# Windowed attention with a split-precision FFN: other places for the score divisions, the pair loads and the y weight sums

## The chip, the cores and the metric

The kernel runs on one core of one Trainium2 chip. The metric is device time in microseconds (us) of one execution; the time before is the median of three runs. TensorE is called PE (its weight loads PEld), VectorE DVE, ScalarE ACT, GpSimd POOL and the sync engine SP, as in the profile. SP issues every DMA of this kernel from one in-order queue.

## What is computed

```python
# attention: q, k, v are (8, 8, 576, 64)
scores = scale * np.matmul(q, k.transpose(0, 1, 3, 2))
rel = pos[:, None] - pos[None, :]
mask_plain = (rel >= 0) & (rel < 32)                       # heads 0 to 3
mask_dil = (rel >= 0) & (rel < 128) & (rel % 4 == 0)       # heads 4 to 7
attn = exp(scores - max) / (sum + 1e-9);  out = attn @ v
# FFN: x is the attention output as (4608, 512), d_ff is 2048
h = x @ w_in
g = np.maximum(h, 0.0) + alpha * np.minimum(h, 0.0)
y = g @ w_out
```

## The kernel before, in words

Every fp32 product is made of three fp32r matmuls (high·high, high·low, low·high), so each operand needs a high part (a cast, on ACT) and a low part (a subtraction, on DVE). The FFN has 9 token tiles of 512 and 16 blocks `f` of 128 hidden rows. A product of 128x128x512 with its three passes over four chunks is 12 matmuls.

**Slices.** The first three token tiles run in 48 slices, numbered `n` in the two loops of the main program (the second loop starts at L1347). Slice `n` issues on PE `ffn_h` of the next slice (12 matmuls, L488), `ffn_y` of the previous one (12 matmuls, L536), and, where the tables `score_at` and `value_at` name a pair, `scores` (72 small matmuls, L266) and `values` (76, L361) of attention pairs: 32 pairs of batch and two heads, of which pairs 8 to 23 belong to slices 20 to 46. DVE makes `ffn_parts` (L508, L509) and `ffn_low` (L519), the division and transpose of the pair scored one slice earlier (`divisions` L338 to L340, `turns` L346), `maxima` (L318, L321) and half of the evacuation (`lows`, L422); ACT makes `ffn_high` (L514), `exponentials` (L331) and the other half (`highs`, L415). The tiles for k, q and v of a pair have one buffer each, so the load of the next pair (`load_qk` L236/L237, `load_v` L246) can start only when the scores, or the values, of the present one have run.

**Weight sums.** From tile 3 on the FFN uses a seven-product scheme for 2x2 blocks (Strassen-Winograd), which needs sums of weight blocks. They are made ahead, in the slices: `combine` (input weights, eight sums, POOL L586 and L589; cast on ACT L594, low part on DVE L599, two stores L601) and `others` (output weights, POOL L611 and L613; ACT L617, DVE L621, four stores L624). Four of the eight output sums are made in slices; `second_sums` makes the other four later: numbers 4 and 5 on POOL in the first h phase (L1055, L1057, L1065), numbers 6 and 7 on DVE in the y phase behind it. In slices 20 to 35 `save` also stores the split weights, four DMAs a slice.

**Paired stage.** Tiles 3 to 8 run as three pairs of tiles, each in two groups of hidden blocks, so six times an **h phase** (`phase_h`) and a **y phase** (`seven_y`). An h phase has four units `i`; each has the products 1, 7, 6, 2, 5, and while unit `i` runs, the products 3 and 4 of unit `i-1` are put behind its product 1. A product is 6 matmuls (L718). `snap`, `negative` and `high` are ACT's, `add`, `value`, `term` and `low` DVE's. Product 2 of a unit takes the PSUM bank that product 7 and 4 of the unit before filled, so it waits for that unit's `add(21)` on DVE (L770). The hook table of `attention_hooks` puts the last eight pairs into the first four h phases, two into each: a hook `(i, p)` runs behind product `p` of unit `i`. The steps of a pair are scores with maxima, exponentials of five and of four blocks, `middle` (divisions and transpose on DVE), and `end` (values on PE, L308, then evacuation and the store `keep`, L225).

All engines run in the order in which the program is written (a manual schedule); there is no planner.

```python
for u, follows, at in zip(two, (two[1], None), (0, 2)):
    first = (0, 1) if at == 0 else (1, 5)
    hooks[first].append(lambda u=u, follows=follows: scores(u, follows))
    hooks[at, 6].append(lambda u=u: u.exponentials(0, 5))
    hooks[at, 5].append(lambda u=u: u.exponentials(5))
    hooks[at + 1, 4].append(lambda u=u: middle(u))
    hooks[at + 1, 6].append(lambda u=u, follows=follows: end(u, follows))
```

Of the kernel before, what the change touches and what calls it, by code (L numbers as in the profile page):

```python
# [66 lines left out]
def tile_window_attention_prelu_ffn(  # L67
# [528 lines left out]
    def combined_low(i):  # L596
# [3 lines left out]
        for a, w in enumerate((hi, lo)):  # L600
            nc.sync.dma_start(out=wS[i, 3:7, :, a].rearrange("q p n -> p q n"), in_=w.bitcast(F32))  # L601
# [3 lines left out]
    def others(i):  # L605

        sums_of["y"] = t = const.tile([P, 4, 2, 2, P], F32, tag="xA0", name=f"ysum_{i}")
        for j in range(2):
            hi, lo = (
                weight(1, a, 2 * i + j).bitcast(F32).rearrange("p (q c n) -> p q c n", q=2, c=2) for a in range(2))  # L610
            nc.gpsimd.tensor_tensor(out=t[:, 2 * j:2 * j + 2, :, 1], in0=hi, in1=lo, op=ALU.add)  # L611
        for out, x, y, op in ((3, 1, 3, ALU.add), (1, 0, 1, ALU.subtract), (0, 3, 0, ALU.subtract), (2, 2, 0, ALU.subtract)):
            nc.gpsimd.tensor_tensor(out=t[:, out, :, 1], in0=t[:, x, :, 1], in1=t[:, y, :, 1], op=op)  # L613

    def others_high():
        t = sums_of["y"]
        nc.scalar.copy(out=t[:, :, :, 0].bitcast(F32R), in_=t[:, :, :, 1])  # L617

    def others_low(i):
        t = sums_of["y"]  # L620
        nc.vector.tensor_tensor(  # L621
            out=t[:, :, :, 1].bitcast(F32R), in0=t[:, :, :, 1], in1=t[:, :, :, 0], op=ALU.subtract)
        for q in range(4):
            nc.sync.dma_start(  # L624
                out=wY[i, q].rearrange("p c a n -> p (c a n)"), in_=t[:, q].rearrange("p c a n -> p (c a n)"))

    sums_of = {}
# [239 lines left out]
    def phase_h(t, grp, hooks):  # L867
# [15 lines left out]
        for i in range(GP):  # L883
# [12 lines left out]
            u.mm(7)  # L896
            if last:
# [23 lines left out]
    def seven_y(t, grp, us, hooks):  # L921
# [107 lines left out]
    )  # L1029

    def second_sums(in_h, in_y):


        for i, k, loaded, fetches, added, cast, last, stores in SUMS:
            room, to = [], in_h if loaded is None else in_y

            def fetch(c, i=i, k=k, room=room):
                if c == 0 and type(k) is int:
# [468 lines left out]
```

## Time and profile before

| what | value |
|---|---|
| median of 3 runs (lowest, highest) | 920.37 us (919.35, 920.66) |
| the profiled execution | 920.85 us |
| its span, first to last instruction | 918.9 us |
| mean granted TensorE clock | 0.969 of full speed |
| busy: PE, DVE, ACT, POOL | 845.7, 666.7, 453.1, 89.0 us |
| DMA moved | 192.79 MB, 210 GB/s on average |

The profiled execution is 1.95 us longer than its span and 0.48 us above the median. Times inside the trace count from the span's start. Rows of a busy PE do not say that it runs at its peak: what PE lost is read from idle time in front of its instructions and from the granted clock.

### The profile page before, as it was taken

What the parts mean: (1) busy time and instruction counts of PE and PEld (TensorE: products, weight loads), DVE (VectorE), ACT (ScalarE), POOL (GpSimd) and SP (SyncE); (2) the same over time, 40 slices, a digit from 0 to 9 for tenths busy, and PEclk for the clock granted to TensorE, in tenths of its full rate; (3) what the DMA queues carried; (4) which work ended last, traced back from release to release, by engine and by line L of the source; (5) the groups of instructions that cost most, each with busy time, mean ns of one, the idle gap of its engine ahead of it and who ended that gap; (6) DMA issues with size and microseconds to landing.
All of it is one profiled execution on the core that took longest, in us unless ns stands there. A gap on an engine that the chain in (4) does not pass through costs nothing.

```text
span 918.9 us, 20357 instructions
## 1 busy us (share of the span) xinstructions
PE 845.7 (92%) x8014; PEld 687.5 (75%) x8014; DVE 666.7 (73%) x1121; ACT 453.1 (49%) x1240; POOL 89.0 (10%) x88
## 2 busy tenths in 40 slices
PE   7889999989988988977899989898999899999998
PEld 5668888877776777865687778677877788888886
DVE  5987767566676587777775888878457888863894
ACT  7876666344333444455434743564246435642650
POOL 0000000220424464024000000000000000000000
PEclk9999999999999899998899999999999999999999
DMA  7742542387699465685598669765766687666664
GB/s 256 260 167 76 177 164 82 115 294 240 205 292 296 163 224 199 215 292 180 180 317 296 183 191 318 244 178 148 236 194 179 187 288 235 193 194 194 193 188 158
DMA packets 130492, 192.79 MB, mean 210 GB/s; under 512 B 11614, under 2 KB 67550, under 8 KB 130398
## 3 DMA queue, kind: packets, MB, share of 16 engines
q1 hardware_dynamic: 130398, 191.51, 66.1%
q8 instruction: 63, 1.03, 0.5%
q14 instruction: 31, 0.25, 0.1%
HBM read 145.33 MB, written 46.14 MB: 208 GB/s over the span
## 4 chain that ended last, share of the span: by engine, by line
PE 72%; DVE 12%; issue 5%; DMA 5%; ACT 4%; SPq 2%; ACTq 0%; DVEq 0%
PE h L488 13%; PE qA L1016 13%; PE pA L718 11%; PE y L536 10%; PE qC L1016 6%; PE pC L718 5%; PE pB L718 5%; PE qB L1016 3%; PE o L361 3%; PE s L266 2%; DMA q<-qT 2%; DVE parts_w L703 1%; PE o L308 1%; DVE raw_xB L697 1%; DVE py L945 1%
## 5 line engine op out<-in xcount | busy, mean ns | idle before, releaser
L488 PE MATMUL h<-x,w_dt.float32r 128*128 128x512 f32 x576 | 144.7, 401 | 3.6 <-DVE pr L318 2.7
L536 PE MATMUL y<-g,w_dt.float32r 128*128 128x512 f32 x576 | 138.5, 390 | 0.0
L488 PEld LDWEIGHTS h<-x,w_dt.float32r 128*128 128x128 f32 x576 | 109.1, 192 | 27.4 <-DVE pr L318 2.9
L536 PEld LDWEIGHTS y<-g,w_dt.float32r 128*128 128x128 f32 x576 | 108.0, 188 | 22.4
L331 ACT ACTIVATE pr<-pr,nm 128x64 f32<-128x64 f32 x216 | 72.4, 339 | 49.5 <-DVE nm L321 49.5
L763 ACT COPY stage<-pA 128x512 f32<-128x512 f32 x72 | 41.8, 580 | 62.2 <-PE pA L718 60.4
L514 ACT CAST g<-m 128x512 fp32r<-128x512 f32 x48 | 29.7, 619 | 70.8 <-DVE m L509 67.9
L718 PE MATMUL pA<-parts_w,ring_w 128*128 128x512 f32 x234 | 58.4, 392 | 0.0
L827 ACT CAST gp<-held 128x512 fp32r<-128x512 f32 x60 | 36.7, 624 | 43.1 <-DVE held L823 42.4
L718 PE MATMUL pA<-parts_w,ring_xA 128*128 128x512 f32 x222 | 55.6, 394 | 0.2 <-ACT stage L763 0.2
L718 PEld LDWEIGHTS pA<-parts_w,ring_w 128*128 128x128 f32 x234 | 44.2, 190 | 9.6
L718 PEld LDWEIGHTS pA<-parts_w,ring_xA 128*128 128x128 f32 x222 | 42.2, 191 | 9.6 <-ACT stage L763 0.6
L508 DVE TENSOR_SCALAR m<-h,al 128x512 f32<-128x512 f32 x27 | 20.2, 749 | 36.0 <-PE h L488 33.5
L519 DVE TENSOR_TENSOR g<-m,g 128x512 fp32r<-128x512 f32 x48 | 34.3, 715 | 12.5 <-ACT g L514 12.4
L770 DVE TENSOR_TENSOR stage<-pC,stage 128x512 f32<-128x512 f32 x48 | 33.0, 687 | 14.1 <-ACT stage L763 13.8
L777 DVE SCALAR_TENSOR_TENSOR held<-held,bal,stage 128x512 f32<-128x512 f32 x42 | 31.9, 758 | 14.6 <-ACT held L807 14.0
L1016 PE MATMUL qA<-gp,ring_xA 128*128 128x512 f32 x174 | 42.4, 390 | 0.0
L331 ACT ACTIVATION_READ_ACCUMULATOR pr<-pr,nm 128x1 f32 x216 | 41.0, 190 | 0.0
L832 DVE TENSOR_TENSOR gp<-held,gp 128x512 fp32r<-128x512 f32 x60 | 40.3, 679 | 0.0
L941 ACT COPY py<-qA 128x512 f32<-128x512 f32 x24 | 13.8, 587 | 52.2 <-PE qA L1016 48.0
L1016 PE MATMUL qA<-gp,ring_w 128*128 128x512 f32 x162 | 39.5, 389 | 0.0
L308 PE MATMUL o<-lasting_pt,lasting_v 32*64 32x64 f32 (+1 forms) x672 | 11.0, 276 | 30.3 <-issue 20.5
(193 smaller groups left out, 1746.2 us busy)
## 6 DMA issues: line engine op xcount, KB each, us to landing
ring_w<-wS SPq DMA_DIRECT2D x69, 256.0 KB, 2.8
ring_xA<-wS SPq DMA_DIRECT2D x66, 256.0 KB, 3.0
ring_xA<-wY SPq DMA_DIRECT2D x40, 256.0 KB, 2.9
ring_w<-wY SPq DMA_DIRECT2D x36, 256.0 KB, 3.0
ring_g<-wS SPq DMA_DIRECT2D x33, 256.0 KB, 3.0
wO<-w_dt.float32r SPq DMA_DIRECT2D x32, 256.0 KB, 4.4
wS<-wc SPq DMA_DIRECT2D x16, 512.0 KB, 4.1
ring_w<-wO SPq DMA_DIRECT2D x31, 256.0 KB, 3.1
```

Source lines behind the costliest of these rows:

```text
L331: nc.scalar.activation(out=self.pr[:, r, :], in_=self.ps[r // CUT0][:, r % CUT0, :] if self.onto else self.pr[:, r, :], func=AF.Exp, bias= ...
L488: nc.tensor.matmul(ms[t, f], lhsT=weight(0, a, f)[:, c * P:(c + 1) * P], rhs=half(t, c)[:, e, :], start=(c == 0 and n == 0), stop=(c == NC ...
L514: nc.scalar.copy(out=g[:, 0, :], in_=ms[t, f])
L519: nc.vector.tensor_tensor(out=g[:, 1, :], in0=ms.pop((t, f)), in1=g[:, 0, :].bitcast(F32), op=ALU.subtract)
L536: nc.tensor.matmul(ys[t][c], lhsT=weight(1, a, f)[:, c * P:(c + 1) * P], rhs=g[:, e, :], start=(first and n == 0), stop=(last and n == 2),)
L718: nc.tensor.matmul(to, lhsT=w[:, (2 * a + c) * P:(2 * a + c + 1) * P], rhs=part_of(name, e)[:, c * TT:(c + 1) * TT], start=start and c == ...
L763: nc.scalar.copy(out=self.s(n), in_=self.A)
L770: nc.vector.tensor_tensor(out=self.s(n), in0=getattr(self, src), in1=self.s(to), op=ALU.add)
L777: nc.vector.scalar_tensor_tensor(out=self.m[n], in0=self.m[n], scalar=bal[:, f:f + 1], in1=self.at(n), op0=ALU.mult, op1=ALU.add)
L827: nc.scalar.copy(out=self.pair(n)[:, 0], in_=self.whole(n))
L832: nc.vector.tensor_tensor(out=p[:, 1], in0=self.whole(n), in1=p[:, 0].bitcast(F32), op=ALU.subtract)
L1016: nc.tensor.matmul(to(q)[c], lhsT=w[:, k * P:(k + 1) * P], rhs=rhs[:, e], start=(i, q) in firsts and n == 0, stop=i == GP - 1 and n == 2, ...
```

## The change

Four parts. (1) In the h phases, the first pair's `middle` goes from behind product 4 of unit 1 to behind product 1, its `end` from product 6 to product 7; the second pair's scores, exponentials, `middle` and `end` go from (1,5), (2,6), (2,5), (3,4), (3,6) to (1,2), (2,1), (2,6), (2,5), (3,4). The hooks of product 5 now run in front of `negative(11)` and `add(22)`. (2) In the slices, `load_qk` of the next pair is issued directly behind the scores and `load_v` directly behind the values; before, both stood at the end of the slice. `keep` goes to the end of the next slice, the stores of `combine` to the end of their own. (3) `others` makes six of the eight output sums in slices (32, 34, ... 42, cast two slices later) in a tile with two halves; the high part gets a tile of its own from the five that rotate for `g`, the low part is made behind the last exponentials, and the store, now eight DMAs of 128 KB, one slice later. `second_sums` keeps numbers 6 and 7. (4) The eight `combine` slices move from 21, 23, 31, ... 41 to 21, 23, 25, 31, ... 39.

```diff
     def others(i):
-        sums_of["y"] = t = const.tile([P, 4, 2, 2, P], F32, tag="xA0", name=f"ysum_{i}")
+        if not ysums:
+            ysums.append(const.tile([P, 2, 4, 2 * P], F32, tag="xA0", name="ysums"))
+        t = ysums[0][:, len(ysums) % 2]
+        ysums.append(t)
...
+        sums_of[i] = t
+    def others_high(i):
+        high = gbuf([P, 4, 2 * P], F32R, f"wd{i}")
+        nc.scalar.copy(out=high, in_=sums_of[i])
+        sums_of[i] = high, sums_of[i]
     def others_low(i):
+        high, t = sums_of[i]
+        nc.vector.tensor_tensor(out=t.bitcast(F32R), in0=t, in1=high.bitcast(F32), op=ALU.subtract)
+    def others_store(i):
+        for a, t in enumerate(sums_of[i]):
+            for q in range(4):
+                nc.sync.dma_start(
+                    out=wY[i, q, :, :, a], in_=(t if a else t.bitcast(F32))[:, q].rearrange("p (c n) -> p c n", c=2))
...
             u.mm(7)
+            also(7)
...
             u.add(11)
+            also(2)
...
             u.snap(3)
+            also(5)
             u.negative(11)
             u.add(22)
             more(5)
-            also(5)
...
     SUMS = (
-        (4, "xC0", None, ((0, 1), (0, 1), (0, 4), (0, 4)), (1, 1), (2, 1), (2, 1), ((2, 4), (2, 6))),
-        (5, "xC1", None, ((0, 6), (0, 5), (1, 1), (1, 4)), (2, 1), (2, 5), (3, 1), ((3, 4), (3, 6))),
...
+        steps = ((0, 1), (0, 6), (0, 5), (1, 1), (1, 7)), ((1, 2), (2, 1), (2, 6), (2, 5), (3, 4))
...
-    for k, n in enumerate((21, 23, 31, 33, 35, 37, 39, 41)):
+    for k, n in enumerate((21, 23, 25, 31, 33, 35, 37, 39)):
...
-    for k, n in enumerate((32, 35, 38, 41)):
+    for k, n in zip((4, 5, 0, 1, 2, 3), range(32, 44, 2)):
         other_at[n] = cast_at[n + 2] = k
...
         if scored:
             scored.scores()
+            pairs[pairs.index(scored) + 1].load_qk()
         if valued:
             valued.values()
+            pairs[pairs.index(valued) + 1].load_v()
         if n in split_at:
             combined_low(split_at[n])
-        if n in cast_at:
-            others_low(cast_at[n])
+            put[n].append(lambda i=split_at[n]: combined_store(i))
...
-            valued.keep()
+            put[n + 1].append(valued.keep)
         if scored:
             scored.exponentials(5)
-        for u in pairs[2 * NC:AHEAD + 1]:
...
+        if n in cast_at:
+            others_low(cast_at[n])
+            put[n + 1].append(lambda i=cast_at[n]: others_store(i))
...
+        for op in put.pop(n, ()):
+            op()
```

**DVE, second h phase, behind product 5 of unit 0.** `pC` and `stage` are product bank and snapshots, `held` the values, `rs` the inverse row sums, `pr` the exponentials, `lasting_pt` their transpose. Before, from `add(22)` to the transpose:

```order
L770 TENSOR_TENSOR stage_5846<-pC_1_0_5806,stage_5835 128x512
L777 SCALAR_TENSOR_TENSOR held_4975<-held_4975,bal,stage_5835 128x512
L777 SCALAR_TENSOR_TENSOR held_5000<-held_5000,bal,stage_5846 128x512
L777 SCALAR_TENSOR_TENSOR held_5011<-held_5011,bal,pA_1_0_5751 128x512
L770 TENSOR_TENSOR stage_5846<-pC_1_0_5806,stage_5759 128x512
L832 TENSOR_TENSOR split_xB_5013<-held_4975,split_xB_5013 128x512
L777 SCALAR_TENSOR_TENSOR held_5026<-held_5026,bal,stage_5846 128x512
L338 TENSOR_SCALAR rs_2_5887<-sums_79 128x9
L339 RECIPROCAL rs_2_5887<-rs_2_5887 128x9
L340 TENSOR_TENSOR pr_78<-pr_78,rs_2_5887 128x576
L346 STREAM_TRANSPOSE lasting_pt<-pr_78 128x576
```

Now:

```order
L781 TENSOR_TENSOR stage_5869<-pC_1_0_5825,stage_5854 128x512
L338 TENSOR_SCALAR rs_2_5881<-sums_79 128x9
L339 RECIPROCAL rs_2_5881<-rs_2_5881 128x9
L340 TENSOR_TENSOR pr_78<-pr_78,rs_2_5881 128x576
L346 STREAM_TRANSPOSE lasting_pt<-pr_78 128x576
L788 SCALAR_TENSOR_TENSOR held_5023<-held_5023,bal,stage_5854 128x512
L788 SCALAR_TENSOR_TENSOR held_5043<-held_5043,bal,stage_5869 128x512
L788 SCALAR_TENSOR_TENSOR held_5054<-held_5054,bal,pA_1_0_5770 128x512
L781 TENSOR_TENSOR stage_5869<-pC_1_0_5825,stage_5778 128x512
L843 TENSOR_TENSOR split_xB_5056<-held_5023,split_xB_5056 128x512
L788 SCALAR_TENSOR_TENSOR held_5069<-held_5069,bal,stage_5869 128x512
```

The four instructions of the division and transpose stand in front of six others that they stood behind; the second row from the end but one (`add(21)`, from bank `pC`) now stands behind them.

**SP, slice 22** (`ob` is the finished output of tile 1, k_2 and q_2 belong to the pair scored in slice 23). Before:

```order
L549 DMA out<-ob_15_0_2116 128x512
L549 DMA out<-ob_15_1_2117 128x512
L549 DMA out<-ob_15_2_2118 128x512
L549 DMA out<-ob_15_3_2119 128x512
L246 DMA v_1_2238<-vW 128x640
L236 DMA k_2_2240<-kT 128x576
L237 DMA q_2_2241<-qT 128x576
```

Now:

```order
L236 DMA k_2_2170<-kT 128x576
L237 DMA q_2_2171<-qT 128x576
L246 DMA v_1_2214<-vW 128x640
L549 DMA out<-ob_15_0_2116 128x512
L549 DMA out<-ob_15_1_2117 128x512
L549 DMA out<-ob_15_2_2118 128x512
L549 DMA out<-ob_15_3_2119 128x512
```

The three loads stand in front of the four stores, and k and q in front of v.

**POOL, from its last sums of the slices to its end** (`wsum` are input weight sums, `ysum` and `ysums` output weight sums, `wy` the sums of `second_sums`). Before:

```order
L586 TENSOR_TENSOR wsum_xA_3243<-w_3_dt.float32r 128x512 x2
L589 TENSOR_TENSOR wsum_xA_3243<-wsum_xA_3243 128x256 x4
L611 TENSOR_TENSOR ysum_4358<-w_3_dt.float32r 128x4x128 x2
L613 TENSOR_TENSOR ysum_4358<-ysum_4358 128x2x128 x4
L1055 TENSOR_TENSOR wy_4884<-wy_4884 128x8x128
L1057 TENSOR_TENSOR wy_4884<-wy_4884 128x2x128 x4
L1065 TENSOR_TENSOR wy_4884<-wy_4884 128x8x128
L1055 TENSOR_TENSOR wy_4950<-wy_4950 128x8x128
L1057 TENSOR_TENSOR wy_4950<-wy_4950 128x2x128 x4
L1065 TENSOR_TENSOR wy_4950<-wy_4950 128x8x128
```

Now:

```order
L586 TENSOR_TENSOR wsum_xA_3255<-w_3_dt.float32r 128x512 x2
L589 TENSOR_TENSOR wsum_xA_3255<-wsum_xA_3255 128x256 x4
L616 TENSOR_TENSOR ysums<-w_0_dt.float32r 128x512 x2
L619 TENSOR_TENSOR ysums<-ysums 128x256 x4
L616 TENSOR_TENSOR ysums<-w_3_dt.float32r 128x512 x2
L619 TENSOR_TENSOR ysums<-ysums 128x256 x4
```

The instructions on `wy` are gone from POOL, and it ends with the sums of the slices.

## Rows read from the trace of the kernel before

**Rows 1.** The page, busy time, share and instructions of each engine.

```profile
PE 845.7 (92%) x8014; PEld 687.5 (75%) x8014; DVE 666.7 (73%) x1121; ACT 453.1 (49%) x1240; POOL 89.0 (10%) x88
```

**Rows 2.** Waits of PE: engine, line, released by: us in total, times, longest.

```profile
PE o L308 <- issue: 20.5, 5, 4.7
PE s L266 <- DMA q<-qT: 11.9, 5, 3.8
PE o L308 <- DVE lasting_pt L346: 9.8, 3, 5.3
PE pB L718 <- DVE stage L770: 5.4, 4, 4.6
```

**Rows 3.** Stretches of slices 23, 33, 36 to 38, 40, 44: length, busy us, PEclk, DMA.

```profile
core 0: us, PE busy (x) PEld busy (x) DVE busy (x) ACT busy (x) POOL busy (x), PEclk, DMA share, GB/s
180.67:194.03 13.36, 9.60 (x177) 8.11 (x173) 8.91 (x18) 6.97 (x31) 4.64 (x6) 0.87 0.84 279
262.92:275.41 12.49, 9.72 (x177) 8.21 (x173) 9.09 (x18) 5.65 (x26) 4.06 (x5) 0.86 0.91 303
289.45:303.35 13.90, 9.50 (x173) 7.81 (x173) 7.62 (x15) 5.85 (x32) 11.36 (x12) 0.85 0.76 240
303.35:310.18 6.83, 6.83 (x26) 5.53 (x25) 2.95 (x7) 2.39 (x11) 0.00 (x0) 0.80 0.48 158
310.18:318.13 7.95, 7.95 (x173) 6.61 (x171) 7.13 (x11) 2.89 (x5) 5.13 (x4) 1.00 0.73 256
323.71:334.58 10.87, 8.10 (x173) 6.61 (x171) 9.98 (x11) 3.57 (x4) 9.32 (x8) 1.00 0.36 127
353.71:366.24 12.53, 9.00 (x173) 7.56 (x172) 10.63 (x14) 4.61 (x5) 1.14 (x1) 0.91 0.78 275
```

**Rows 4.** Timeline in the slices: start, us, instruction, [idle before it <- releaser].

```profile
178.25 1.21 PE L266 MATMUL s<-k,q 64*32 64x64 f32 x72
...
185.61 0.45 SPq L237 DMA_DIRECT2D q<-qT  x1
...
190.17 2.15 PE L266 MATMUL s<-k,q 64*32 64x64 f32 x72 [3.76 <-DMA q<-qT]
```

**Rows 5.** Stretches of h phases 1 to 5, columns as in rows 3.

```profile
384.75:446.56 61.81, 47.20 (x469) 37.65 (x468) 43.55 (x64) 29.03 (x82) 17.16 (x12) 0.86 0.69 227
...
487.39:536.45 49.06, 42.01 (x469) 33.68 (x468) 34.83 (x67) 27.93 (x85) 0.00 (x0) 0.97 0.65 207
...
577.25:628.78 51.53, 43.65 (x470) 34.81 (x468) 39.14 (x67) 27.92 (x80) 0.00 (x0) 0.93 0.60 184
...
669.58:720.31 50.73, 43.66 (x470) 34.83 (x469) 34.80 (x65) 27.94 (x85) 0.00 (x0) 0.93 0.59 166
...
761.13:797.26 36.13, 35.92 (x158) 29.07 (x157) 29.99 (x45) 21.33 (x38) 0.00 (x0) 1.00 0.73 219
```

**Rows 6.** Timeline of the second h phase, which starts at 487.39, columns as in rows 4.

```profile
502.44 0.17 DVE L338 TENSOR_SCALAR rs<-sums 128x9 f32<-128x9 f32 x1
...
504.57 1.10 PE L308 MATMUL o<-lasting_pt,lasting_v 32*64 32x32 f32 x84 [2.27 <-issue]
...
516.87 1.66 PE L718 MATMUL pB<-parts_w,ring_w 128*128 128x512 f32 x6 [0.27 <-DVE stage L770]
...
521.25 0.69 DVE L770 TENSOR_TENSOR stage<-pC,stage 128x512 f32<-128x512 f32 x1
...
527.02 0.68 DVE L770 TENSOR_TENSOR stage<-pC,stage 128x512 f32<-128x512 f32 x1
...
531.20 1.52 PE L308 MATMUL o<-lasting_pt,lasting_v 32*64 32x32 f32 x84 [4.51 <-issue]
```

**Rows 7.** Timeline of the first h phase, POOL and DVE.

```profile
416.97 2.81 POOL L1055 TENSOR_TENSOR wy<-wy 128x1024 f32<-128x1024 f32 x1
...
417.48 2.84 DVE L823 TENSOR_TENSOR held<-held,held 128x512 f32<-128x512 f32 x1
```

**Rows 8.** Group of instructions: names, shapes, count | busy us, mean ns | idle before.

```profile
L621 DVE TENSOR_TENSOR ysum<-ysum 128x1024 fp32r<-128x1024 f32 x4 | 5.2, 1304 | 0.1
```

More of the change, by code (lines that the diff above doesn't have):

```diff
@@ L1024, in tile_window_attention_prelu_ffn, with second_sums, sums @@
     SUMS = (
[4 rows of a table removed]
-    )
-    def second_sums(in_h, in_y):
-        for i, k, loaded, fetches, added, cast, last, stores in SUMS:
-            room, to = [], in_h if loaded is None else in_y
+        (6, 1, (5, 6, 7, 8), 15, 20, 22, (24, 25)),
+        (7, 3, (10, 11, 12, 13), 20, 22, 24, (27, 28)),
+    )
+    def second_sums(hooks):
+        for i, k, fetches, added, cast, last, stores in SUMS:
+            room = []
             def fetch(c, i=i, k=k, room=room):
-                if c == 0 and type(k) is int:
+                if c == 0:
                     room.extend(gbuf([P, 2, 2, 2, P], F32, f"wy{i}_{n}", k + n) for n in range(2))
-                elif c == 0:
-                    room.append(const.tile([P, NC, 2, 2, P], F32, tag=k, name=f"wy{i}"))
-                n = NC // len(room)
                 nc.sync.dma_start(
-                    out=room[c // n][:, c % n].rearrange("p o a n -> p (o a n)"),
+                    out=room[c // 2][:, c % 2].rearrange("p o a n -> p (o a n)"),
                     in_=wO[i // GP, c, i % GP].rearrange("p o a n -> p (o a n)"))
             def block(room, q):
-                t, a = (room[q % 2], 0) if len(room) == 2 else (room[0], q % 2 * 2)
-                return t[:, a:a + 2, q // 2, 1]
-            engine = nc.gpsimd if loaded is None else nc.vector
-            def sums(room=room, engine=engine):
+                return room[q % 2][:, :, q // 2, 1]
+            def sums(room=room):
                 for t in room:
-                    engine.tensor_tensor(out=t[:, :, :, 1], in0=t[:, :, :, 0], in1=t[:, :, :, 1], op=ALU.add)
+                    nc.vector.tensor_tensor(out=t[:, :, :, 1], in0=t[:, :, :, 0], in1=t[:, :, :, 1], op=ALU.add)
                 for out, x, y, op in ((3, 1, 3, ALU.add), (1, 0, 1, ALU.subtract), (0, 3, 0, ALU.subtract), (2, 2, 0, ALU.subtract)):
-                    engine.tensor_tensor(out=block(room, out), in0=block(room, x), in1=block(room, y), op=op)
+                    nc.vector.tensor_tensor(out=block(room, out), in0=block(room, x), in1=block(room, y), op=op)
             def high(room=room):
@@ L1076, in second_sums @@
             for c in range(NC):
-                to[fetches[c]].append(lambda c=c, fetch=fetch: fetch(c))
-            to[added].append(sums)
-            to[cast].append(high)
-            to[last].append(low)
+                hooks[fetches[c]].append(lambda c=c, fetch=fetch: fetch(c))
+            hooks[added].append(sums)
+            hooks[cast].append(high)
+            hooks[last].append(low)
             for half in range(2):
-                to[stores[half]].append(lambda half=half, store=store: store(half))
+                hooks[stores[half]].append(lambda half=half, store=store: store(half))
     def reload(t, c):
@@ L1125, in end @@
             u.keep()
-        for u, follows, at in zip(two, (two[1], None), (0, 2)):
-            first = (0, 1) if at == 0 else (1, 5)
-            hooks[first].append(lambda u=u, follows=follows: scores(u, follows))
-            hooks[at, 6].append(lambda u=u: u.exponentials(0, 5))
-            hooks[at, 5].append(lambda u=u: u.exponentials(5))
-            hooks[at + 1, 4].append(lambda u=u: middle(u))
-            hooks[at + 1, 6].append(lambda u=u, follows=follows: end(u, follows))
+        steps = ((0, 1), (0, 6), (0, 5), (1, 1), (1, 7)), ((1, 2), (2, 1), (2, 6), (2, 5), (3, 4))
+        for u, follows, at in zip(two, (two[1], None), steps):
+            for n, op in zip(at, (
+                    lambda u=u, follows=follows: scores(u, follows), lambda u=u: u.exponentials(0, 5),
+                    lambda u=u: u.exponentials(5), lambda u=u: middle(u),
+                    lambda u=u, follows=follows: end(u, follows))):
+                hooks[n].append(op)
     def paired_stage():
@@ L1140, in paired_stage @@
                 if (t, grp) == (NSTD, 0):
-                    second_sums(in_h, in_y)
+                    second_sums(in_y)
                 two, todo = todo[:2], todo[2:]
```

43 lines of the change are left out of this document (16 added, 27 removed), and 2 rows, old and new, of the table SUMS.

## Prediction

> **What bounds the kernel now.** I read the busy line first: PE is busy 92% of the span, DVE 73% [rows 1]. So PE is the bound, and a change pays where PE stands idle or runs at half clock. PE's waits [rows 2] name the places. Before the values of the h phases (L308) it waits 20.5 + 9.8 = 30.3 us in eight places, once for each pair of these phases; "issue" there can't be the whole cause, because the transpose that the values read comes late on DVE (below). Before the scores of the slices (L266) it waits 11.9 us for `q`, in five places. Before product 2 it waits 5.4 us for DVE's snapshot (L770).
>
> The windows then tell what a wait costs beyond itself. A clean slice with scores and values takes 7.95 us at PEclk 1.00. Slices 23, 33 and 36 hold the same PE work and take 13.36, 12.49 and 13.90, at 0.85 to 0.87 [rows 3]: behind a gap PE runs for a while at the lower of its two clock levels (1.2 instead of 2.4 GHz), and in rows 3 slice 37, which has no idle time at all (6.83 busy of 6.83), still ran at 0.80. The h phases read the same way: the fifth, without attention, takes 36.13 at 1.00; the first four take 61.81, 49.06, 51.53 and 50.73 at 0.86 to 0.97 [rows 5].
>
> **Part 1, the h phases.** What must PE do in one? The 36.13 of the fifth phase, and two pairs: scores of 1.21 [rows 4] and values of 1.10 [rows 6] each, so 36.13 + 2 x 2.31 = 40.7 us. That is the floor at full clock; the four phases lie 213.13 - 4 x 40.7 = 50.3 above it.
>
> First values, in the second phase (start 487.39) [rows 6]. The division started at 502.44, 15.05 after the start; PE's values ran at 504.57, 2.13 later, after 2.27 idle, so PE was there at 14.91. In the changed order the division stands in front of six DVE instructions of 128x512, 6 x 0.68 = 4.1, so it may start at 10.95 and PE can begin at 13.08. PE gets there one product earlier (1.66 by the product in rows 6), at 13.25. The gap closes, with little to spare.
>
> What is late next is `add(21)`: product 2, at 516.87, waited 0.27 for it. The DVE instructions that stand ahead of it are the same set as before, only in another order, so it comes sooner only as far as DVE had idle time to fill. PE, however, comes 2.27 sooner. Between no such filling (wait 0.27 + 2.27 = 2.5) and full filling (0.3) I take about half: 1.2.
>
> Second values: they ran at 531.20 after 4.51 of idle [rows 6], so PE was there at 526.69, and by the same 2.13 the division had started at 529.07. In the changed order it stands, right behind an `add` of the unit before, eight DVE instructions of 128x512 sooner, next to the one that ran at 521.25. From there 2.13 more is 523.38. PE gets to the values two products sooner, 526.69 - 2 x 1.66 = 523.37, and the 2.27 of the first gap sooner than that, less the 1.2 that it now waits: 522.3. DVE too runs ahead where it waited for PE. I take the gap as gone, and 1.1 as the most that stays. `add(21)` of that unit ended at 527.02 + 0.68 = 527.70; PE arrives at product 2 behind it sooner by about what it saved, and I take another wait of 0.9, by the same bounds of 0.3 and 2.5. At the end the y phase finds DVE's last parts later than PE: nothing to 2, I take 0.9.
>
> So each phase takes 40.7 + 1.2 + 0.9 + 0.9 = 43.7, and the four save 213.13 - 174.8 = **38.3**. The bounds are 46 a phase (both waits at 2.5; saves 29) and the floor (saves 50). By phases that is 18.1, 5.4, 7.8 and 7.0. The first gains most since POOL's 17.16 us of sums [rows 5] leave it: beside a POOL sum of 2.81 a DVE instruction of 128x512, 0.68 elsewhere [rows 6], took 2.84 [rows 7].
>
> **Part 2, the loads.** Before, the scores that free `k` and `q` ended at 178.25 + 1.21 = 179.46, but the `q` load was issued only at 185.61, behind four stores and `v`, and the scores came at 190.17 after 3.76 idle [rows 4]. From issue to use took 4.56. Issued directly behind the scores it would land by about 185; PE wanted it at 190.17 - 3.76 = 186.4. Slices 23, 33 and 36 stand 39.75 - 3 x 7.95 = 15.9 above clean ones [rows 3], waits and clock together; slice 37 loses 6.83 x 0.20 = 1.3 to the clock; the other two waits for `q`, of at most 3.8 each, I put at 2. Of these 19.2 some stay: the window of slice 36 is the longest though `q` cost it no more than 3.8, so other gaps stand in it. Between the bare waits (11.9) and 19.2 I take **16**.
>
> The price of the move: stores and `save` now wait behind loads on SP's queue, and `keep` and the stores of the sums wait a slice. What waits for the stores is a tile that is written again: one slice of about 8 us stands between, and a load took 4.56. The cover is that slice; without it, the price is the fourth rival below.
>
> **Parts 3 and 4, the sums.** Slice 40 takes 10.87 and slice 44 12.53 for the work of 7.95; DVE is busy 9.98 and 10.63 of it, with a low part of 1.30 (L621) in front of the maxima [rows 3, 8]. Behind the last exponentials it no longer holds them: 1.3 in slice 40; in slice 44, 4.6 lost with the clock at 0.91, of which I take 3. Bounds 0 and 7.5; taken **4.3**. Against that stand two more sums in the slices: on POOL two times six instructions, at the 9.32 / 8 of slice 40 [rows 3] some 14 us; on DVE 2 x 1.30 [rows 8]; on ACT two casts of about as much. A clean slice with 5.13 us of POOL beside 7.13 of DVE took 7.95 [rows 3], so DVE and POOL have room there; eleven sums fill nearly every slice from 31 to 42 now. Bounds 0 and 3 (both low parts wholly on the path); taken **1**.
>
> Does POOL hold DVE off? One DVE instruction was stretched by 2.84 - 0.68 = 2.16 beside a POOL sum [rows 7]; the clean slice shows four POOL instructions costing PE nothing. The Trainium skill ("SBUF — State Buffer", section "SBUF: two separate sides") speaks against the change here: DVE and GpSimd share a port pair, which one of them holds for its whole instruction while the other blocks, also where a DVE instruction with two SBUF inputs meets a GpSimd one that reads SBUF. The trace agrees with it in rows 7, and by it alone every added sum could cost a DVE instruction its length.
>
> **Sum.** 38.3 + 16 + 4.3 - 1 = 57.6. The span goes from 918.9 to 861.3; the profiled execution is 1.95 longer than its span, 863.3; it was 0.48 above the median, so the median becomes about **863 us**. A difference under 0.2% (1.8 us) can hardly be told from none.
>
> **The rivals.**
> - *DVE takes the h phases' gain back* (0.16). If DVE has hardly any idle time ahead of `add(21)`, the gap before the values comes back before product 2, and the clock falls there instead. For it: product 2 waits already, 5.4 us in four places, once 4.6 [rows 2]. Against: DVE is busy 34.83 of 49.06 [rows 5]. Phases 2 to 4 then gain 3 each, the first 15: 24 instead of 38.3, so 877.
> - *`q` is late anyway* (0.12). In slices 23 and 33 the DMA engines are busy 84% and 91%, at 279 and 303 GB/s [rows 3]: then it isn't the issue that is late, but the transfer, which shares the engines with the same stores. The slices with late loads gain 4 instead of 16: 875.
> - *POOL holds DVE in the slices* (0.07). Eleven sums from slice 31 on, each with one DVE instruction of the chain to the maxima stretched by 2.16 [rows 7], is 11 x 2.16 = 24 us. Less the two sums of the first h phase, about 22 net: 885. Rows 3 speak against it (7.95 with POOL busy 5.13). The Trainium skill's rule on the shared port pair ("SBUF — State Buffer", "SBUF: two separate sides") is the one that would do this.
> - *Slower: the stores hold ACT* (0.02). The high part of a y sum now gets one of the five tiles that rotate for `g`; ACT's cast must wait until the earlier store from that tile has landed, and behind it on ACT stand the exponentials and `ffn_high`, for which PE waits. Six sums are cast. To eat 57.6 us, each cast must hold PE 9.6 us, more than a clean slice; at 20 us each the kernel takes 863 + 120 = 983, and it is slower from 9.6 on. For it: the stores are eight DMAs now, behind others on SP's queue, with DMA shares up to 0.91 [rows 3]. Against: a load took 4.56 us at such a share.
> - *Better than the range* (0.03): no new waits in the h phases, and every late slice clean, 50 + 24: about 847.
>
> The forecast keeps 0.60. **The range, 849 to 884**, takes in the first two rivals, the bounds of part 1 (851 and 872, by 50 and 29) and those of the slices; outside are the third rival's upper half, the slower case and the best one. The slower case, and half a point for one like it, give slower by over 0.2%: 0.025; within 0.2%, only if several of these meet: 0.01; the rest, faster by over 0.2%: 0.965.
>
> **What would show it.** Idle before L308 falls from 30.3 to under 3, and waits for `q` from 11.9 to under 3. The first four h phases take 42 to 45 us each, at PEclk 0.98 or more. Product 2 waits 1 to 2 us a phase for the snapshot, more than now. POOL is idle in the first h phase. Slices 23, 33, 36 and 44 come down to 8 to 10. I am wrong if the waits before product 2 or before the y phase grow past 3 us a phase, if `q` still lands after 190 in slice 23, or if slices 31 to 43, clean before, now show DVE instructions of over 2 us and `scores` or `ffn_h` waiting behind them.

## The result, and the profile after

| | before | after |
|---|---|---|
| median (lowest to highest) | 919.86 us (917.04 to 920.66) | 863.42 us (861.41 to 865.51) |
| profiled execution | 920.85, span 918.9 | 864.97, span 863.2 |
| mean granted clock | 0.969 | 0.997 |

The ratio of the times is 0.9392, 95% interval 0.9357 to 0.9426: 6.1% faster. The median stands within half a microsecond of the forecast of 863. That is closer than the working deserves: in the h phases two of the three forecast waits did not come and one came that was not forecast, and the largest term of the slices has a second cause that the prediction did not have. The experiments show both.

PE is now busy 96% of a shorter span, against 92% in [rows 1] (page, busy line of the kernel after):

```profile
PE 826.8 (96%) x8014; PEld 668.9 (77%) x8014; DVE 664.4 (77%) x1123; ACT 455.8 (53%) x1240; POOL 87.6 (10%) x88
```

PE does the same 8014 matmuls in 18.9 us less busy time, because fewer of them run at the lower clock. POOL has lost no work: its sums moved into the slices. The waits of PE, kernel after (us in all, times, longest), answer to [rows 2]:

```profile
PE o L361 <- issue: 6.2, 5, 2.1
PE h L488 <- DVE pr L318: 5.2, 7, 1.6
PE pC L729 <- DVE stage L781: 5.1, 4, 1.3
PE pB L729 <- DVE stage L781: 4.6, 4, 1.4
```

The 30.3 us in front of the values (L308) and the 11.9 us for `q` are gone from the list. What has taken their place is small: DVE's snapshots in the h phases, 5.1 and 4.6 us, and the maxima's DVE work in front of the next slice's `ffn_h`, 5.2 us. The longest row, 6.2 us in front of the values of the slices (L361), was 7.3 before; no run looks into it.

The windows of slices 23, 33, 36, 40 and 44 after (length, busy us by engine, PEclk, DMA share, GB/s), as in [rows 3]:

```profile
179.69:188.63 8.94, 8.18 (x177) 6.72 (x173) 7.61 (x16) 5.57 (x22) 0.38 (x1) 1.00 0.96 320
255.53:264.54 9.01, 8.23 (x177) 6.72 (x173) 8.80 (x18) 5.01 (x22) 0.38 (x1) 1.00 1.02 331
279.75:288.16 8.41, 8.16 (x173) 6.72 (x173) 6.77 (x13) 5.01 (x22) 7.33 (x8) 1.00 0.86 267
...
307.29:316.11 8.82, 8.09 (x174) 6.61 (x172) 7.92 (x11) 4.09 (x5) 6.82 (x6) 1.00 0.86 265
336.58:346.39 9.81, 8.09 (x173) 6.61 (x171) 7.56 (x11) 4.19 (x5) 0.00 (x0) 1.00 0.60 179
```

All five run at full clock. Slices 23 and 33 move 320 and 331 GB/s, where [rows 3] has them waiting at 279 and 303: the DMA engines had not been at their limit.

The h phases 1 to 4 after, as in [rows 5]:

```profile
365.94:409.69 43.75, 41.03 (x469) 32.38 (x468) 34.48 (x63) 27.73 (x80) 0.00 (x0) 1.00 0.65 203
450.49:493.96 43.47, 41.10 (x470) 32.38 (x468) 33.19 (x65) 28.41 (x85) 0.00 (x0) 1.00 0.68 218
534.97:579.62 44.65, 41.32 (x469) 32.43 (x468) 37.85 (x66) 28.52 (x80) 0.00 (x0) 1.00 0.66 201
620.42:663.90 43.48, 41.11 (x469) 32.39 (x468) 33.14 (x63) 28.48 (x85) 0.00 (x0) 1.00 0.61 180
```

The first four took 213.13 us and take 175.35: 37.8 saved, where the forecast had 38.3. From the start of slice 20 to that of slice 46 it was 211.91 us and is 194.07, 17.8 saved (forecast 19.3); these two stretches, as windows of the kernel before and then of the kernel after:

```profile
160.46:372.37 211.91, 190.66 (x2918) 157.76 (x2916) 144.25 (x257) 87.50 (x361) 71.67 (x72) 0.96 0.69 224
```

```profile
159.48:353.55 194.07, 185.47 (x2917) 152.39 (x2916) 150.91 (x259) 88.92 (x363) 87.36 (x84) 0.99 0.82 256
```

In what follows "the slices" is this stretch. The stretch ahead of it, which the change does not touch, took 158.2 to 162.1 us in the profiles of this study; that is most of the spread between executions, so effects of a few microseconds are read from the windows and not from the medians.

### The profile page after: what moved, and what is told of

It reads as the page before. It is cut to its first block, busy times and chain, and to the rows that moved or that the text cites. A ratio compares the mean times of both kernels' runs of the same rounds, so it can differ in the third digit from the quotient of the medians.

```text
span 863.2 us, 20404 instructions
## 1 busy us (share of the span) xinstructions
PE 826.8 (96%) x8014; PEld 668.9 (77%) x8014; DVE 664.4 (77%) x1123; ACT 455.8 (53%) x1240; POOL 87.6 (10%) x88
## 4 chain that ended last, share of the span: by engine, by line
PE 76%; DVE 15%; ACT 4%; issue 3%; DMA 2%; SPq 0%; ACTq 0%; DVEq 0%
PE qA L1029 14%; PE h L488 13%; PE pA L729 12%; PE y L536 11%; PE pC L729 6%; PE qC L1029 6%; PE qB L1029 3%; PE pB L729 3%; PE o L361 2%; PE s L266 1%; ACT pr L331 1%; DVE pr L340 1%; DVE py L958 1%; PE idle L127 1%; DVE m L508 1%
## 5 line engine op out<-in xcount | busy, mean ns | idle before, releaser
L519 DVE TENSOR_TENSOR g<-m,g 128x512 fp32r<-128x512 f32 x48 | 35.8, 745 | 14.0 <-ACT g L514 13.8
L958 DVE TENSOR_TENSOR py<-qC,py 128x512 f32<-128x512 f32 x24 | 16.0, 688 | 31.0 <-PE qC L1029 24.7
L1029 PEld LDWEIGHTS qA<-gp,ring_xA 128*128 128x128 f32 x174 | 32.4, 188 | 7.5 <-DVE gp L843 0.5
```

The costliest lines, as they stand in the source:

```text
L519: nc.vector.tensor_tensor(out=g[:, 1, :], in0=ms.pop((t, f)), in1=g[:, 0, :].bitcast(F32), op=ALU.subtract)
L1029: nc.tensor.matmul(to(q)[c], lhsT=w[:, k * P:(k + 1) * P], rhs=rhs[:, e], start=(i, q) in firsts and n == 0, stop=i == GP - 1 and n == 2, ...
```

## The experiments

**Part 1 alone, on the kernel before.**

```diff
-        for u, follows, at in zip(two, (two[1], None), (0, 2)):
...
+        steps = ((0, 1), (0, 6), (0, 5), (1, 1), (1, 7)), ((1, 2), (2, 1), (2, 6), (2, 5), (3, 4))
...
             u.mm(7)
+            also(7)
...
             u.add(11)
+            also(2)
...
             u.snap(3)
+            also(5)
             u.negative(11)
             u.add(22)
             more(5)
-            also(5)
```

> The kernel before with part 1 alone (new places of the hooks in the h phases; loads, sums and combines as before). Theory (the forecast's account): the gaps before the values come from the place of the divisions alone, so h phases 2 to 4 fall from 49.1, 51.5 and 50.7 to 43.5 to 44.7 each, 19 to 20 us together, and the idle time before L308 there is under 1 us; the first h phase keeps POOL's sums and DVE instructions stretched to over 2 us, and falls from 61.8 only to 50 to 55. Kernel 889 to 896 us. Rival (the steps alone do it all, POOL's sums cost the first phase nothing): the first phase at 44 to 46 too, kernel 881 to 886. Second rival (what DVE is relieved of comes from the other parts): phases 2 to 4 stay over 47, kernel over 905.

Measured: 892.18 us, ratio 0.9695 (0.9664 to 0.9725). The first two h phases in its windows (the third took 44.68, the fourth 43.56):

```profile
384.59:436.68 52.09, 44.77 (x469) 34.17 (x468) 43.08 (x62) 28.64 (x81) 18.33 (x12) 0.93 0.71 245
477.50:521.03 43.53, 41.16 (x469) 32.39 (x468) 33.18 (x65) 28.38 (x85) 0.00 (x0) 1.00 0.69 220
```

Phases 2 to 4 are those of the full change to a tenth: the places of the hooks do all of it there. The first still takes 52.09, 8.3 more than in the kernel after, and its POOL and DVE rows (timelines of this run) show why:

```profile
408.91 2.59 POOL L1067 TENSOR_TENSOR wy<-wy 128x1024 fp32r<-128x1024 f32 x1 [3.72 <-ACT wy L1063]
411.45 2.85 POOL L1057 TENSOR_TENSOR wy<-wy 128x1024 f32<-128x1024 f32 x1
```

```profile
409.76 2.28 DVE L832 TENSOR_TENSOR split_xB<-held,split_xB 128x512 fp32r<-128x512 f32 x1
411.97 2.88 DVE L777 SCALAR_TENSOR_TENSOR held<-held,bal,stage 128x512 f32<-128x512 f32 x1
```

Two DVE instructions, 0.68 and 0.75 elsewhere, take 2.28 and 2.88 just while POOL runs over 1024 elements; product 2 then waits 5.40 us. So of the first phase's 18.1 us, 9.7 are the steps' and 8.3 come with POOL's sums leaving it, if the steps are taken first; the next run gives the split in the other order.

**Part 1 undone, in the kernel after** (the diff above, reversed).

> The changed kernel with part 1 undone (hooks at their old places). Theory: h phases 2 to 4 back at 49 to 51.5, and the first, with POOL's sums gone from it, like them at 49 to 51: 863 + 26 = 887 to 892 us, clock in the second halves back at one half behind gaps of 4.5 us. Rival (the first phase's 18 us were the steps', not POOL's): first phase at 57 to 62, kernel 897 to 901.

Measured: 889.55 us, ratio 0.9658 (0.9617 to 0.9699), 26.1 above the kernel after. The first two phases (then 51.35 and 49.04):

```profile
364.51:414.92 50.41, 43.39 (x469) 34.67 (x468) 35.91 (x64) 27.13 (x80) 0.00 (x0) 0.93 0.64 193
455.73:507.26 51.53, 44.51 (x469) 35.65 (x468) 35.01 (x67) 27.92 (x85) 0.00 (x0) 0.90 0.65 200
```

The first phase, free of POOL, is like the others. Against 61.81 before and 43.75 after, POOL's leaving is worth 11.4 us here and the steps 6.7: the two overlap, and neither split is the only one. The lengths sum to 202.33, 27.0 above those of the kernel after; from the side of the kernel before, part 1 was worth 29.3. Taken by itself from either side, the step of part 1 held.

**The loads undone, and then the stores too.** First the loads of `k`, `q` and `v` alone go back to the end of the slice:

```diff
             scored.scores()
-            pairs[pairs.index(scored) + 1].load_qk()
...
             valued.values()
-            pairs[pairs.index(valued) + 1].load_v()
...
+        for u in pairs[2 * NC:AHEAD + 1]:
...
+            if due[0]:
+                u.load_qk()
+            if due[1]:
+                u.load_v()
```

> The changed kernel with the loads of k, q and v back at the end of the slice, behind the stores of finished outputs; all else changed. Theory: the scores wait for q again, 9 to 13 us in four to six places, with the clock loss behind them 13 to 19 us in slices 22 to 46: 876 to 882 us. Rival (the slices gained because stores and sums moved, the loads are early enough in either place once keep and the sums' stores stand a slice later): waits for q under 4 us, 863 to 868 us.

Measured: 872.08 us, ratio 0.9469 (0.9432 to 0.9505), between the theory and the rival; each holds in some of the slices. `q` is late three times, not five, in the slices 23, 27 and 33 (PE's waits in this run):

```profile
PE s L266 <- DMA q<-qT: 8.0, 3, 3.6
```

These three took 13.69, 9.86 and 11.53 us, about as long as before the change (13.36, 9.82 and 12.49). Slices 36 and 37, which the prediction had counted among those with late loads, took 8.95 and 5.56, as good as clean. So in a second run the stores went back to their old places in their own slices as well:

```diff
-            put[n].append(lambda i=split_at[n]: combined_store(i))
+            combined_store(split_at[n])
...
-            put[n + 1].append(valued.keep)
+            valued.keep()
...
-            put[n + 1].append(lambda i=cast_at[n]: others_store(i))
+            others_store(cast_at[n])
```

> The changed kernel with the loads back at the end of the slice (as in the run with the loads undone, 872 us, three waits for q, 8.0 us) and the stores of attention outputs and sums back in their own slices, in front of the loads. Theory (of the gain in slices 36 and 37, 6 us, the store's place is the cause: a load behind the stores waits for them on SP's queue): the wait for q returns in slice 36 and perhaps in others, 10 to 13 us in all, 876 to 882 us. Rival (slices 36 and 37 gained from where the sums and their low parts stand): no fourth wait for q, 870 to 874 us.

Measured: 890.66 us, ratio 0.9648 (0.9605 to 0.9691), more than the theory's 876 to 882. The slices took 218.49 us, against 203.41 with the loads alone undone and 194.07 in the kernel after; slice 36 took 17.08. PE's waits:

```profile
PE s L266 <- DMA q<-qT: 18.2, 6, 6.2
...
PE s L266 <- ACT wd L624: 2.9, 1, 2.9
```

The queue in front of slice 36's `q`, in the timeline of SP:

```profile
284.73 2.59 SPq L634 DMA_DIRECT2D wY<-wd  x4
287.42 2.55 SPq L634 DMA_DIRECT2D wY<-ysums  x4
290.02 2.15 SPq L570 DMA_DIRECT2D wS<-w_dt.float32r  x1
...
293.97 1.64 SPq L604 DMA_DIRECT2D wS<-wc  x2
295.72 1.27 SPq L225 DMA_DIRECT2D kept<-kept  x1
297.08 1.14 SPq L246 DMA_DIRECT2D v<-vW  x1
298.28 0.80 SPq L236 DMA_DIRECT2D k<-kT  x1
299.13 0.48 SPq L237 DMA_DIRECT2D q<-qT  x1
```

The eight stores of a y sum, the four of `save`, the two of the input sums and `keep` all stand in front of the load, and issuing them takes nearly all of the time from 284.73 to 296.99. `q` goes out at 299.13, and the scores start at 304.33 after 6.22 idle. In the kernel after, the `q` for slice 36 went out at 277.32. With the stores later, early loads are worth 9.3 us in the slices; with the loads late, the later stores are worth 15.1. No run has early loads with the stores in their old places, so whether early loads alone would have kept slice 36 clean stays open. Nor are the 15.1 a gain over the kernel before: there four y sums were made in slices, with four stores each, and here it is six with eight. The wait for `wd` (ACT's cast of a y sum) does not show the prediction's fourth rival: the cast began at 337.63 right behind another cast, without a wait for a store, and `q`, issued at 334.55, was on its way until about the same time (the scores began at 338.69; 4.56 us from issue to use in [rows 4]).

**The low part of the y sums back in front of the maxima.**

```diff
         if n in split_at:
             combined_low(split_at[n])
...
+        if n in cast_at:
+            others_low(cast_at[n])
         if scored:
             scored.maxima()
...
         if n in cast_at:
-            others_low(cast_at[n])
             put[n + 1].append(lambda i=cast_at[n]: others_store(i))
```

> The changed kernel with the low part of the y sums (DVE, 1.3 us) back in front of the maxima; all else changed. Theory: it holds the maxima and so the h product of the next slice and the exponentials, up to 1.3 to 1.75 us in each of the six slices in which it stands, where PE has no slack: 3 to 6 us, 866 to 869 us. Rival (what slices 40 and 44 gained came from the places of the combines and from the early loads): 862 to 865 us, gaps before L488 as in the changed kernel (5.2 us in all).

Measured: 869.19 us, ratio 0.9446 (0.9409 to 0.9482). The waits in front of `ffn_h` double, from 5.2 to:

```profile
PE h L488 <- DVE pr L318: 10.7, 9, 1.9
```

The slices took 197.50, 3.4 above the kernel after, and 5.0 above its second execution (below). The theory's cause holds, with the median just above its range.

**The combines at their old slices.**

```diff
-    for k, n in enumerate((21, 23, 25, 31, 33, 35, 37, 39)):
+    for k, n in enumerate((21, 23, 31, 33, 35, 37, 39, 41)):
```

> The changed kernel with the eight combines at their old slices (21, 23, 31, 33, 35, 37, 39, 41 instead of 21, 23, 25, 31, 33, 35, 37, 39). Theory: slice 27 falls from 8.6 to 8.0, but slice 43 gets a cast and a low part on top of the last y sum's cast in 44, with the pairs' values in both: slices 43 to 45 grow by 1 to 3 us together, 864 to 867 us. Rival (the place of the combines is worth nothing, slice 44 gained by the low part's place alone): 862 to 864 us.

Measured: 867.48 us, ratio 0.9407 (0.9371 to 0.9443). The slices took 195.43. Slice 27 falls to 8.09 as expected; the loss is in slice 44, 13.11 against 9.81, and it is a gap in front of the values:

```profile
341.99 1.21 PE L266 MATMUL s<-k,q 64*32 64x64 f32 x72
347.34 2.30 PE L361 MATMUL o<-pt,v 32*64 32x32 f32 x76 [4.14 <-DVE m L509]
```

DVE is busy without a pause from 335.30 to 343.56 in this run, with that combine's low part (1.75 us) among the operands of tile 3 that it makes there; behind that it waits 1.11 us for ACT, as it does in the kernel after, and only then makes the `m` (L509) that releases the values. They wait 4.14 us and then run at the lower clock (2.30 us instead of 1.35). The low part is only about half of it: POOL's sums run beside DVE from 335.30 to 340.21, and three DVE instructions there (L338, L340, L519) take 0.95, 1.11 and 1.23 us, against 0.17, 0.76 and 0.69 in the kernel after, where POOL had ended by 333.71.

**POOL's second steps left out.** The sums that are stored lack these steps.

```diff
-        for out, x, y, op in ((3, 2, 3, ALU.add), (4, 3, 0, ALU.subtract), (2, 0, 2, ALU.subtract), (1, 1, 4, ALU.subtract)):
+        for out, x, y, op in ((4, 3, 0, ALU.subtract),):
...
-        for out, x, y, op in ((3, 1, 3, ALU.add), (1, 0, 1, ALU.subtract), (0, 3, 0, ALU.subtract), (2, 2, 0, ALU.subtract)):
-            nc.gpsimd.tensor_tensor(out=t[:, out], in0=t[:, x], in1=t[:, y], op=op)
```

> The changed kernel with most of POOL's second steps left out: three of the four half-size instructions of each of the eight input sums and all four of each of the six output sums (so the sums that are stored lack these steps; casts, low parts and stores stay). POOL's busy time falls from 88 to some 45 us. Theory (the forecast's price of the sums: about nothing on PE's path): the slices shorten by less than 3 us, 861 to 864 us, while DVE instructions beside POOL get shorter. Rival (POOL holds DVE off where it is on PE's path, the forecast's third rival): the gaps before L488 (5.2 us) and the DVE work before the maxima shrink and slices 23 to 45 lose 4 us or more: 855 to 859 us.

Measured: 862.76 us, ratio 0.9347 (0.9309 to 0.9384). The slices:

```profile
160.87:351.47 190.60, 183.85 (x2918) 151.38 (x2916) 145.15 (x259) 89.20 (x363) 44.57 (x36) 1.00 0.84 259
```

With POOL busy 44.57 instead of 87.36, DVE is busy 5.8 us less for the same 259 instructions: POOL does stretch DVE in the slices. But PE gets back only 1.9 to 3.5 us (against the two executions of the kernel after, 194.07 and 192.48). That is for half of POOL's work. For the whole of it, by proportion, it would be some 4 to 7 us (an estimate from these two lengths and POOL's busy times), against the 22 of the prediction's third rival.

**The kernel after once more,** on the chip of the last three.

> The changed kernel once more, word for word, on the same chip as the three others of this set. All theories: 861 to 866 us; slices 22 to 46 and the h phases as before, so what differs between two executions lies in the first 160 us (the start of slice 20 came between 158.2 and 162.1 in the runs so far).

Measured: 864.72 us, ratio 0.9379 (0.9337 to 0.9422); its slices took 192.48, and the differences between slices of the two executions are below 0.7 us but for slice 45: 5.57 against 7.16, because `ffn_h` ran at the lower clock in the first execution (4.60 us, against 3.01). Where a length is compared with both executions, 1.6 us of the difference are this.

**Three edits on what is left.** For three of PE's waits in the kernel after, an order can be changed. The first is the second pair's division, which goes behind `add(22)`:

```diff
             u.negative(11)
             u.add(22)
+            also(22)
...
-((1, 2), (2, 1), (2, 6), (2, 5), (3, 4))
+((1, 2), (2, 1), (2, 6), (2, 22), (3, 4))
```

> The changed kernel with the second pair's division and transpose (four DVE instructions, 2.0 us) behind add(22) instead of in front of it. Theory: the wait of product 3 for that snapshot in bank pC (1.3 us in each of the four phases, 5.1 in all) was made by the order alone and goes; the transpose ends 0.65 us later, still ahead of PE's values: each phase 1.2 shorter (42.3 to 42.5), kernel 858 to 860 us. Rival (DVE has no slack there): the wait comes back in front of the values (L308), over 3 us in all, kernel 862 to 865 us.

Measured: 864.62 us, ratio 0.9372 (0.9307 to 0.9438), outside the theory's range; the median shows nothing. In the profiled execution the stretch ahead of slice 20, 162.11, is 2.6 longer than in the kernel after. The windows show more: the phases took 43.11, 42.95, 43.93 and 42.98, 2.4 us less together, of 5.1 that the wait had cost. The wait in front of `pC` is gone and none is in front of the values, so the rival's cause falls. But PE, 1.3 us sooner, now meets `add(21)` a second time:

```profile
PE pB L729 <- DVE stage L781: 6.0, 8, 1.5
```

Eight waits where there were four. Next the DVE instruction that stands in front of `add(21)` and itself waits some 1.2 us for ACT:

```diff
     def third(u):
...
-        u.value(12)
...
     def fourth(u):
         u.mm(4)
         u.add(21)
+        u.value(12)
```

> The changed kernel with value(12), which waits some 1.2 us for ACT's negative(12), behind add(21) instead of in front of it. Theory: product 2's wait for add(21) (0.96 to 1.43 us in each of the four phases, 4.6 in all) is made by DVE standing idle for ACT in front of it, not by too much work on DVE; it falls to 0.3 or less: kernel 859 to 861 us. Rival (DVE is the bound of that stretch): value(12) now comes late, and what it feeds (the term T1 and bank pA) makes PE or ACT wait as long elsewhere: 862 to 865 us, and waits on L729 of 9 to 10 us in all as in the changed kernel.

Measured: 861.32 us, ratio 0.9335 (0.928 to 0.939). The waits for `add(21)`, 4.6 us, are gone altogether, but 3.3 us more of waiting stand in two other places, where the kernel after has 5.1 and 0.2:

```profile
PE pC L729 <- DVE stage L781: 5.8, 4, 1.5
...
PE pA L729 <- ACT stage L774: 2.8, 5, 0.9
```

The phases took 43.28, 42.99, 44.09 and 43.01, 2.0 less together. The third edit is in the slices:

```diff
-        if n in split_at:
-            combined_low(split_at[n])
-            put[n].append(lambda i=split_at[n]: combined_store(i))
         if scored:
             scored.maxima()
+        if n in split_at:
+            combined_low(split_at[n])
+            put[n].append(lambda i=split_at[n]: combined_store(i))
+        if scored:
             scored.exponentials(0, 5)
```

> The changed kernel with the low part of the combined input sums (DVE, 1.2 us in eight slices) behind the maxima instead of in front of them. Theory: PE's waits in front of L488 for the maxima's DVE work (5.2 us in seven slices) come from this instruction: under 2 us left, kernel 859 to 861 us. Rival (the evacuations behind it hold the next slice as long, or the gaps come from POOL's stretch of other DVE instructions): the waits only move, 862 to 865 us.

Measured: 862.16 us, ratio 0.9342 (0.9287 to 0.9396). The waits in front of `ffn_h` fall from 5.2 to 1.6 us and the slices to 190.56, 1.9 to 3.5 less than in the two executions of the kernel after. In the profiled execution the stretch ahead of slice 20, 161.26, is 1.8 longer than in the kernel after, and the median, 1.3 below, does not show the gain clearly.

The three diffs together:

> The changed kernel with the three edits of the runs before in this set together. Theory (each wait has its own cause): the gains add, 4.8 + 4 + 3 = 12, kernel 850 to 854 us. Rival (in the h phases the waits hang together, so that one that goes hands its time to the next): 855 to 860 us.

Measured: **853.92 us**, ratio 0.9258 (0.9205 to 0.931): faster than the kernel after, whose interval begins at 0.9357. The first two h phases (then 42.90 and 41.93):

```profile
362.35:404.43 42.08, 40.95 (x470) 32.40 (x469) 33.74 (x62) 26.78 (x79) 0.00 (x0) 1.00 0.68 210
445.25:487.16 41.91, 41.12 (x469) 32.39 (x468) 32.56 (x65) 27.57 (x84) 0.00 (x0) 1.00 0.69 223
```

The four sum to 168.82, 6.5 below the kernel after, where the two edits alone gave 2.4 and 2.0: here the waits do hang together, but the other way than the rival said. Alone, each edit handed part of its gain to waits further on: 1.4 us to a second `add(21)` in the one, 0.7 to `pC` and 2.6 to ACT's snapshots in the other. With both, two thirds of the 9.7 us of both waits are gained. Waits for DVE's snapshots are gone from the list of this run, and 0.5 to 0.9 us a phase for ACT's is what is left.

## Why the prediction was right, and where it was not

**Part 1.** The floor of 40.7 us stands: PE is busy 41.0 to 41.3 us in the four phases, at full clock, and with all three edits a phase comes down to 41.9. The gap before the first values closed: in the second phase of the kernel after, the division started at 460.61, 10.12 after the phase's start (forecast 10.95), and the values ran at 463.95, 13.46 after it (forecast 13.25), without a wait. The rest of that phase:

```profile
478.70 1.66 PE L729 MATMUL pB<-parts_w,ring_w 128*128 128x512 f32 x6 [0.96 <-DVE stage L781]
...
485.73 1.67 PE L729 MATMUL pC<-parts_w,ring_xA 128*128 128x512 f32 x6 [1.28 <-DVE stage L781]
487.33 1.13 PE L308 MATMUL o<-lasting_pt,lasting_v 32*64 32x32 f32 x84
```

The first new wait is the forecast one, in its place and size: product 2 behind `add(21)`, 0.96 (1.43 at most, over the phases) against 1.2. **The second failed in its place.** The prediction put 0.9 at the same product of the next unit. It came earlier, in front of a product into bank `pC`, 1.28, and for another instruction: the second pair's division now stands in front of `add(22)`, which frees that bank. DVE's rows:

```profile
483.08 0.17 DVE L338 TENSOR_SCALAR rs<-sums 128x9 f32<-128x9 f32 x1
...
484.32 0.78 DVE L346 STREAM_TRANSPOSE lasting_pt<-pr 128x576 f32<-128x576 f32 x1
485.03 0.65 DVE L781 TENSOR_TENSOR stage<-pC,stage 128x512 f32<-128x512 f32 x1
```

The prediction had read that the hooks of product 5 now run in front of `add(22)` and asked of it only that the transpose come sooner; it did not ask who waits for what the division was put ahead of. **The third term failed too:** the y phase, given 0.9, waits for nothing. 1.2 + 0.9 + 0.9 and 0.96 to 1.43 + 1.3 + 0 come out nearly alike, and that is luck. The reason behind the first wait was half right: the prediction had DVE's amount of work in mind, but DVE was idle 1.19 us, waiting for ACT, before `value(12)`, the instruction right in front of `add(21)`:

```profile
477.29 0.75 DVE L788 SCALAR_TENSOR_TENSOR between<-between,bal,pA 128x512 f32<-128x512 f32 x1 [1.19 <-ACT between L818]
```

The run with `add(21)` first took the wait away without taking any work off DVE. The first rival, by which DVE takes most of the gain back, did not come: product 2 waits 4.6 us in all four phases, and the clock stays at 1.00.

**The first phase.** The forecast's 18.1 us came, and its reason was right in kind: both the steps and POOL's sums leaving count, 9.7 and 8.3 or 6.7 and 11.4 by the order in which they are taken.

**Part 2** was right in size, and right in cause for three of its slices. Those that it named gave 13.4 (23, 33, 36), 1.2 (37) and 2.3 (27 and 32), 17.0 against 16. In slices 23, 27 and 33 the place of the load is the cause, as forecast: with the loads alone undone `q` is late there again. SP's waits in the kernel before, just ahead of the issue of those three `q` (windows 179:186, 212:219 and 258:268), show what the loads stood behind:

```profile
SPq L549 <- ACT ob L548: 8.3, 1, 8.3
```

```profile
SPq L246 <- PE o L361: 1.9, 1, 1.9
```

```profile
SPq L549 <- DVE ob L544: 5.2, 4, 4.7
```

In slices 23 and 33 it was the output stores (L549), whose data were not ready; the change did not move them, only the loads to in front of them. In slice 27 it was the load of `v`, which waited for the values while `k` and `q` stood behind it. Slice 36 is another case: with the loads late it is clean as long as the stores are later, and late with both undone. The prediction costed the moved stores only as a price, not as a gain, and **that is what it missed**. The kernel before has stores in front of that `q` too (window 279:293):

```profile
SPq L624 <- DVE ysum L621: 2.4, 1, 2.4
```

How the 17.0 us divide between the loads and the stores is not shown, since the run with early loads and old stores is missing; the 9.3 and the 15.1 hold each with the other in the state that its run had.

What SP waits for afterwards, kernel after:

```profile
SPq L236 <- PE s L266: 45.3, 12, 19.3
...
SPq L246 <- PE o L361: 9.9, 9, 4.3
```

Now the queue stands at the load of `k`, waiting for the scores that free its tile, which is the place where waiting is right: the load goes out the moment that it can. The load of `v` had waited 24.0 us for the values before, with `k` and `q` behind it.

**Parts 3 and 4.** Slices 40 and 44 gave 2.05 and 2.72, 4.8 against 4.3, and the runs with the low part early and the combines at their old places give 3.4 and 1.4 by windows (5.8 and 4.1 by medians; 5.0 and 3.0 against the second execution). The price of the sums was set low: slices 24, 35, 42, 43 and 45 lost 3.9 together, where the forecast had 1 and an upper bound of 3. In the second execution, without the lower clock in slice 45, they lost 1.8, and the slices gained 19.4 in all, against a forecast of 19.3. With loads and stores both undone the slices, 218.49, are 6.6 longer than before the change.

**The Trainium skill's rule** ("SBUF — State Buffer", section "SBUF: two separate sides"), by which one of DVE and GpSimd holds a shared port pair for its whole instruction while the other waits, agrees with the rows of POOL and DVE in the first phase (2.85 beside 2.88). The 22 us that the third rival made of it in the slices did not come: they gained 17.8 where the forecast without that rival had 19.3, and with half of POOL's work left out DVE gets back 5.8 us and PE 1.9 to 3.5. Instructions do get stretched; they mostly aren't those that PE is waiting for. In slice 44 of the run with the old combine places they were.

**The second rival, of the DMA engines,** fell: `q` was late by when it was issued. At 320 and 331 GB/s, above the 279 and 303 of the slices in which it had come late, there is no wait for it.

## What to carry to other kernels

In an in-order queue, ask of a load that comes late what stood in front of it, and why. Here it was an output store whose data came late, another load that waited for its tile, or a row of stores whose issue took 12 us; loads can be put forward and stores put back, and here each was worth something with the other as it was. When an instruction is moved forward, ask who waits for each of those that it now stands in front of. And remove waits of one chain together before judging any: two edits that gave 2.4 and 2.0 us alone gave 6.5 together.

## What the runs showed of the hardware

A gap of the same length before the same instruction does not always bring the lower clock. With part 1 undone, PE stood 2.27 us before the values of the first phase and 2.26 before those of the second. The 5 us behind the first gap and behind the second:

```profile
381.70:386.70 5.00, 5.00 (x169) 4.10 (x170) 4.33 (x9) 2.94 (x8) 0.00 (x0) 1.00 0.58 153
472.92:477.92 5.00, 5.00 (x96) 4.25 (x96) 3.51 (x10) 2.20 (x8) 0.00 (x0) 0.68 0.49 142
```

PE is busy all the time in both; it does 169 matmuls at full clock in the one and 96 at a mean of 0.68 in the other. Slice 45 of the two executions of the kernel after is a second case: behind the same two gaps (1.25 or 1.26 us before the values and 0.47 before `ffn_h`) the same matmuls took 4.60 us in one and 3.01 in the other. Nothing in these runs tells why, so what a single gap of this length costs beyond itself could not be forecast, only what such gaps cost on the average of several.
